# Head sums of a dilated attention as 32-column tiles of TensorE, with heads on partitions in the softmax and the weights turned by DMA

## The chip, the cores and the metric

The kernel runs on one core of one Trainium2 chip. A core has TensorE (PE in the profile: matmuls, with PEld its weight loads), VectorE (DVE), ScalarE (ACT), GpSimd (POOL) and SyncE (SP, which here only issues transfers), and 16 DMA engines that all queues share. The metric is the device time of one execution in microseconds (us), the median of several runs.

## What is computed

One token block of 2048 rows of width 512 goes through a layer norm and then through two branches whose results are added to the input. Branch A is attention with 32 heads of width 16, in which each token looks at 8 earlier tokens, two apart. Branch B is a gated unit with a mix over the sequence.

```python
xn = layernorm(x)                                   # x: 2048 x 512
q, k, v = split(xn @ wqkv)                          # 32 heads of 16
idx = pos[:, None] - 2 * arange(8)[None, :]         # masked where idx < 0
logits = einsum('bhsd,bhswd->bhsw', q, k[idx]) * 16 ** -0.5
a = einsum('bhsw,bhswd->bhsd', softmax(logits), v[idx]) @ wo
z = gelu(xn @ w_in)                                 # 2048 x 1792
z1, z2 = z[..., :896], layernorm(z[..., 896:])
g = einsum('ts,bsf->btf', w_sp, z2) + b_sp[:, None]
out = x + a + (z1 * g) @ w_out
```

## The kernel before

Tokens are cut into 16 blocks of 128 (`b`) and 4 waves of 512 (`j`, and `tc` for the columns of `w_sp`). Every step is a `Task` in a `Plan`: an engine, a function that emits its instructions, the tiles that it reads and writes, an estimated duration `est` and a priority `prio` (lower goes first). `schedule()` runs a list scheduler over the tasks with these estimates and with a simple model of the transfers (an issue time on the queue, a bandwidth, a latency), and the order that comes out for each engine is the order in which that engine's instructions are emitted. `emit()` puts semaphore waits where a task depends on another engine's. So the order on every engine, SP's queue included, is fixed when the kernel is built; on the chip an engine waits at the head of its list. A changed estimate can change the order of everything that follows.

The steps that the change and the prediction touch, with the lines of the kernel before:

- Dummy matmuls (L536 to L541): `NWARM` = 22 matmuls on a tile of zeros, of the lowest priority (`prio` 1000). The first 10 have 512 columns, the other 12 have 128. They read `zeros`, which DVE sets at L492.
- `ln_block` (L550 to L587): statistics and normalization of a block on DVE and POOL. The first 4 blocks are turned by TensorE (L572, evicted by ACT at L578), the other 12 by DMA transposes on SP (L584).
- `v_block` (L589), `qk_pair` (L608), `z2_block` (L689), `z1_group` (L732): the projections. V goes to DRAM (L605). Q and K are laid out with (head, part of the head's width) on partitions: 4 chunks `c` of 4 values of each head, so that partition p belongs to head p // 4.
- `prods` (L627): for each wave, DVE multiplies Q with K shifted by 0, 2, ... 14 tokens (L635, 128 x 4096) for each chunk and adds the 4 products (L640). `pb` then holds, for each of 8 shifts `w`, 512 tokens, and the 4 partitions of a head still have to be summed. TensorE does it with `E32`, a 128 x 32 matrix of zeros and ones (L643 to L652): for each of 4 blocks and 8 shifts the stationary operand is a 128 x 128 piece of `pb`, the moving one is `E32` with 32 columns, so tokens come out on partitions and heads in the columns. That is 32 matmuls in a wave, in two tasks `red`.
- `softmax` (L655 to L687): a mask for the first tokens (first wave only), maximum, subtraction on DVE, exponential on ACT, sum in three steps, reciprocal, and a product (L684) that writes the weights to `attn`, tokens on partitions.
- `pv_block` (L839): for each block the 8 shifted copies of V are loaded from DRAM (L845, 1 MB on SP, 4 slots), multiplied with the weights (L850) and added up (L853, L856) on DVE, and the result is turned by a DMA transpose on SP (L859) into `OT`.
- `g_group` (L811): `w_sp` comes in by 16 DMA transposes on SP (L795), 4 to a wave, in 3 slots of which the third shares its memory with `pb`. 448 matmuls of 512 columns (L822), eviction on ACT (L830), bias and product on DVE (L833, L836).
- `out_block` (L864): 4 matmuls with `wo` (L878) and 7 with `w_out` (L887) for each block, the residual added on DVE (L893), and the store on SP (L898).

The DMA model of the scheduler is this, with `issue` 480 ns for SP and ACT:

```python
xs = max(r + iss + dma_pre, dma_free)
xe = xs + t.dma["nbytes"] / (bw if xs > 7000.0 else min(bw, 265.0))
dma_free = xe
t.end = xe + dma_lat
```

Of the kernel before, what the change touches and what calls it, by code (L numbers as in the profile page):

```python
# [14 lines left out]
NEG_BIG = -1.0e9  # L15
# [21 lines left out]
class Plan:  # L37
# [83 lines left out]
    def schedule(self, dma_bw=300.0, xbar_bw=190.0, dma_lat=1300.0, dma_pre=400.0, issue=None, tol=40.0):  # L121
# [45 lines left out]
        while left:  # L167
# [43 lines left out]
            if t.dma is not None:  # L211
                iss = issue[e]
                t.eng_end = r + iss
                bw = xbar_bw if t.dma.get("xbar") else dma_bw
                xs = max(r + iss + dma_pre, dma_free)
                xe = xs + t.dma["nbytes"] / (bw if xs > 7000.0 else min(bw, 265.0))
                dma_free = xe
                t.end = xe + dma_lat
            else:
                dur = t.est  # L220
                if t.tbl is not None:
                    if tbl is not None and t.tbl != tbl:
                        dur += 1300.0
                    tbl = t.tbl
                t.eng_end = t.end = r + dur
# [103 lines left out]
def build_kernel(nc, A_x, A_wqkv, A_wo, B_x, B_w_in, B_w_sp, B_b_sp, B_w_out, out, report=False, emit=True):  # L329
# [9 lines left out]
    NVS = 4  # L339
    NPB = 3  # L340
    NXT = 4
    NWARM = 22
    x2 = A_x[0]
    o2 = out[0]

# [27 lines left out]

    foff = {}
    fb = 0
    for name, n in (("prime", 4), ("mx", 128), ("Zb", 256), ("Z", 128), ("maskt", 256), ("st6", NB * 6),
                    ("mv", NB * 2), ("vpe", NB), ("rstd", NB), ("s1", NB), ("s2", NB), ("m2", NB), ("msq", NB),
                    ("vpe2", NB), ("rstd2", NB), ("mhalf", 4)):
        foff[name] = fb
        fb += n  # L380
# [5 lines left out]
    with ExitStack() as es:  # L386
# [11 lines left out]
        def Fv(name, n, o2_=0):  # L398
            return fp[:, foff[name] + o2_: foff[name] + o2_ + n]
# [7 lines left out]
        def P(bk, n, o_=0):  # L407
            return ps[:, bk.col(o_): bk.col(o_) + n]
# [71 lines left out]
        ident = A("ident", 128)  # L480
        E32 = A("E32", 32)
        zeros = A("zeros", 512)
        maskt = Fv("maskt", 256)
        mhalf = Fv("mhalf", 4)


# [48 lines left out]

        for wi in range(NWARM):  # L536
            bw = plan.bank("warm%d" % wi)
            n_ = 512 if wi < NWARM - 12 else 128
            T("pe", (lambda bw, n_: lambda t: t.matmul(P(bw, n_), zeros[:, 0:128], zeros[:, 0:n_], start=True,  # L539
                                                       stop=True))(bw, n_),  # L540
              reads=["zeros"], writes=[bw], est=(427.0 if n_ == 512 else 75.0), name="warm%d" % wi, prio=1000)  # L541
# [85 lines left out]
        def prods(j):  # L627
            acc = (0, 2)[j % 2]
            for c in range(4):
                s_ = acc if c == 0 else 1  # L630
                qb = AC(off["QT"] + 2048 * (j % 2) + 512 * c, [[0, 8], [1, 512]])
                kb = AC(off["KT"] + c * (S + KP) + KP + 512 * j, [[-2, 8], [1, 512]])
                pbv = A("pb", 4096, 4096 * s_).rearrange("p (w s) -> p w s", w=8)
                rd = [("QT", c, j % 2), ("KT", c, j), ("KT", c, j - 1) if j > 0 else ("KTpad", c)]
                T("dve", (lambda pbv, qb, kb: lambda v: v.tensor_tensor(pbv, qb, kb, ALU.mult))(pbv, qb, kb),  # L635
                  reads=rd, writes=[("pb", s_)], est=c_tt(4096), name="prod%d_%d" % (j, c), prio=5 + j)
                if c > 0:
                    av = A("pb", 4096, 4096 * acc)
                    bv = A("pb", 4096, 4096 * 1)
                    T("dve", (lambda av, bv: lambda v: v.tensor_tensor(av, av, bv, ALU.add))(av, bv),  # L640
                      reads=[("pb", 1)], writes=[("pb", acc)], est=c_tt(4096), name="padd%d_%d" % (j, c), prio=5 + j)
            bk = plan.bank("lg%d" % j, 2)
            for hf in range(2):  # L643
                def mm(t, hf=hf):
                    last = None
                    for blk in range(2 * hf, 2 * hf + 2):
                        for w in range(8):
                            last = t.matmul(P(bk, 32, blk * 256 + w * 32),  # L648
                                            AC(off["pb"] + 4096 * acc + 512 * w + 128 * blk, [[1, 128]]), E32,
                                            start=True, stop=True)  # L650
                    return last
                T("pe", mm, reads=[("pb", acc), "E32"], writes=[bk], est=16 * 27.0, name="red%d_%d" % (j, hf), prio=1)  # L652
            return bk

        def softmax(j, bk):  # L655
            ds = j % 2
            if j == 0:
                T("dve", lambda v: v.tensor_tensor(P(bk, 256), P(bk, 256), maskt, ALU.add),
                  reads=["maskt"], writes=[bk], est=424, name="smask", prio=4)
            T("dve", lambda v: v.tensor_reduce(Fv("mx", 128).rearrange("p (a h) -> p a h", a=4),  # L660
                                               PC(bk.col(), [[256, 4], [1, 32], [32, 8]]), AX.X, ALU.max),
              reads=[bk], writes=["mx"], est=1218, name="smax%d" % j, prio=4)
            T("dve", lambda v: v.tensor_tensor(A("D", 1024, 1024 * ds).rearrange("p (a w h) -> p a w h", a=4, w=8),
                                               PC(bk.col(), [[256, 4], [32, 8], [1, 32]]),
                                               FCa(foff["mx"], [[32, 4], [0, 8], [1, 32]]), ALU.subtract),
              reads=[bk, "mx"], writes=[("D", ds)], est=1222, name="ssub%d" % j, prio=4)
# [3 lines left out]
            T("dve", lambda v: v.tensor_tensor(A("Za", 512).rearrange("p (a w h) -> p a w h", a=4, w=4),  # L670
                                               AC(do, [[256, 4], [32, 4], [1, 32]]),
                                               AC(do + 128, [[256, 4], [32, 4], [1, 32]]), ALU.add),
              reads=[("D", ds)], writes=["Za"], est=c_tt(512), name="sz1_%d" % j, prio=4)
            T("dve", lambda v: v.tensor_tensor(Fv("Zb", 256).rearrange("p (a w h) -> p a w h", a=4, w=2),
                                               AC(off["Za"], [[128, 4], [32, 2], [1, 32]]),
                                               AC(off["Za"] + 64, [[128, 4], [32, 2], [1, 32]]), ALU.add),
              reads=["Za"], writes=["Zb"], est=423, name="sz2_%d" % j, prio=4)
            T("dve", lambda v: v.tensor_tensor(Fv("Z", 128).rearrange("p (a h) -> p a h", a=4),
                                               FCa(foff["Zb"], [[64, 4], [1, 32]]),
                                               FCa(foff["Zb"] + 32, [[64, 4], [1, 32]]), ALU.add),  # L680
              reads=["Zb"], writes=["Z"], est=292, name="sz3_%d" % j, prio=4)
            T("dve", lambda v: v.reciprocal(A("R", 128), Fv("Z", 128)), reads=["Z"], writes=["R"], est=952,
              name="srec%d" % j, prio=4)
            T("dve", lambda v: v.tensor_tensor(AC(off["attn"] + 1024 * j, [[256, 4], [32, 8], [1, 32]]),  # L684
                                               AC(do, [[256, 4], [32, 8], [1, 32]]),
                                               AC(off["R"], [[32, 4], [0, 8], [1, 32]]), ALU.mult),
              reads=[("D", ds), "R"], writes=[("attn", b) for b in range(4 * j, 4 * j + 4)], est=c_tt(1024), name="sattn%d" % j, prio=4)  # L687

        def z2_block(b):  # L689
            bk = plan.bank("z2_%d" % b, 2)  # L690
# [60 lines left out]
        for b in range(8, NB):  # L751
# [13 lines left out]
        T("pool", lambda g: g.memset(maskt, 0.0), writes=["maskt"], est=310, name="mask0", prio=2, after=lnr[:8])  # L765
        for w in range(1, W):
            T("pool", (lambda w: lambda g: g.memset(fp[0:2 * w, foff["maskt"] + 32 * w: foff["maskt"] + 32 * w + 32],
                                                    NEG_BIG))(w), writes=["maskt"], est=120, name="mask%d" % w, prio=2, after=lnr[:8])
# [70 lines left out]
        def pv_block(b):  # L839
# [126 lines left out]
```

## Time and profile before

| What | Value |
|---|---|
| Median of 3 runs | 239.82 us (239.57, 239.82, 241.82) |
| The profiled execution | 239.45 us, of it 238.0 us from the first to the last instruction |
| TensorE matmuls, busy | 233.0 us, 1211 instructions |
| TensorE weight loads, busy | 112.2 us, beside the matmuls |
| VectorE, busy | 213.3 us, 267 instructions |
| ScalarE, busy | 97.6 us |
| GpSimd, busy | 32.4 us |
| L822, matmuls with the 512 columns of `w_sp` | 98.6 us busy |
| L635, L640, L850, VectorE over 128 x 4096 | 36.6, 27.5 and 36.5 us busy |
| DMA | 42.81 MB, mean 180 GB/s |

The table comes from the profile's page. A busy time of TensorE is the union of its matmuls' durations, and these overlap: a matmul of 512 columns is shown with 379 ns, and in a stream the next one starts well before that. Other engines' times can be added up. In the views of the trace each line gives the start and the duration, the engine, the line of the kernel, the operation and its operands; what stands in square brackets is the idle time of the engine just before it and what ended it.

### The profile page before, as it was taken

The page shows a single profiled execution, that of the slowest core. Times are in us where ns is not written, and L with a number is a line of the kernel's source. Part 1 is how long each engine was busy: PE and PEld are TensorE (multiplying, and loading weights), DVE is VectorE, ACT ScalarE, POOL GpSimd, SP SyncE. Part 2 cuts the span into 40 slices and gives each one's busy share as a digit, 9 for nine tenths or more (in the row PEclk, how much of TensorE's full clock was granted, in tenths as well). Part 3 has the DMA queues.
Part 4 walks back from the last instruction along what each step waited for, and adds up shares of the span by engine and source line. Part 5 has one row for each costly group of instructions (what it writes and reads, how often), then busy time and mean ns, then how long its engine had stood idle before and what let it go on. Part 6 is the DMA issues. An engine that isn't in the chain of part 4 may idle for free.

```text
span 238.0 us, 3156 instructions
## 1 busy us (share of the span) xinstructions
PE 233.0 (98%) x1211; PEld 112.2 (47%) x1233; DVE 213.3 (90%) x267; ACT 97.6 (41%) x144; POOL 32.4 (14%) x56
## 2 busy tenths in 40 slices
PE   7999999999999999999999999999999999999996
PEld 3455555555445444544454444444444444444444
DVE  3889989899989899999999999969999999999962
ACT  2587889899889885631112111101010200101110
POOL 2467250501373500000000000000000000000000
DMA  6999969992437100014079999999999998972112
GB/s 178 365 337 192 190 144 200 215 208 74 110 118 250 56 26 18 0 37 142 0 238 313 190 220 264 194 191 254 283 341 348 272 280 264 245 239 66 22 44 66
DMA packets 77805, 42.81 MB, mean 180 GB/s; under 512 B 50128, under 2 KB 77152, under 8 KB 77792
## 3 DMA queue, kind: packets, MB, share of 16 engines
q1 hardware_dynamic: 76480, 40.13, 69.7%
q0 software_dynamic: 800, 2.11, 2.7%
q10 hardware_dynamic: 512, 0.38, 0.5%
q8 instruction: 9, 0.15, 0.3%
q14 instruction: 4, 0.03, 0.0%
HBM read 26.35 MB, written 4.21 MB: 128 GB/s over the span
## 4 chain that ended last, share of the span: by engine, by line
PE 98%; issue 1%; DVE 0%; ACT 0%
PE ps L822 40%; PE ps L614 12%; PE ps L695 10%; PE ps L887 10%; PE ps L739 10%; PE ps L597 6%; PE ps L878 6%; PE ps L539 2%; PE ps L648 1%; PE ps L572 0%; ACT arena L578 0%; DVE arena L893 0%; DVE arena L492 0%
## 5 line engine op out<-in xcount | busy, mean ns | idle before, releaser
L822 PE MATMUL ps<-arena 128*128 128x512 bf16 x441 | 98.6, 379 | 0.4
L822 PEld LDWEIGHTS ps<-arena 128*128 128x128 bf16 x448 | 43.8, 98 | 52.6
L830 ACT ACTIVATE arena<-ps 128x1024 bf16<-128x1024 f32 (+1 forms) x16 | 14.7, 917 | 106.9 <-PE ps L822 96.3
L635 DVE TENSOR_TENSOR arena<-arena 128x4096 bf16<-128x4096 bf16 x16 | 36.6, 2286 | 0.2
L850 DVE TENSOR_TENSOR arena<-arena 128x4096 bf16<-128x4096 bf16 x16 | 36.5, 2284 | 0.0
L853 DVE TENSOR_TENSOR arena<-arena 128x2048 bf16<-128x2048 bf16 (+1 forms) x32 | 30.6, 955 | 0.6
L614 PE MATMUL ps<-arena 128*128 128x512 bf16 x125 | 28.8, 379 | 0.2
L640 DVE TENSOR_TENSOR arena<-arena 128x4096 bf16<-128x4096 bf16 x12 | 27.5, 2289 | 0.2
L887 PE MATMUL ps<-arena 128*128 128x512 bf16 (+2 forms) x117 | 26.9, 366 | 0.1
L695 PE MATMUL ps<-arena 128*128 128x448 bf16 x128 | 26.0, 352 | 0.0
L739 PE MATMUL ps<-arena 128*128 128x512 bf16 x109 | 24.2, 379 | 0.2
L614 PEld LDWEIGHTS ps<-arena 128*128 128x128 bf16 x128 | 14.5, 113 | 13.0
L893 DVE TENSOR_TENSOR arena<-ps,arena 128x512 bf16<-128x512 f32 (+2 forms) x17 | 11.2, 658 | 8.4 <-PE ps L887 7.3
L623 ACT ACTIVATE arena<-ps 128x1024 bf16<-128x1024 f32 x16 | 16.3, 1020 | 4.5 <-PE ps L614 4.3
L695 PEld LDWEIGHTS ps<-arena 128*128 128x128 bf16 x128 | 12.4, 98 | 11.5
L887 PEld LDWEIGHTS ps<-arena 128*128 128x128 bf16 x119 | 11.6, 98 | 12.7
L739 PEld LDWEIGHTS ps<-arena 128*128 128x128 bf16 x112 | 10.8, 98 | 12.7
L745 ACT ACTIVATE arena<-ps 128x1024 bf16<-128x1024 f32 (+1 forms) x16 | 14.1, 916 | 6.1 <-PE ps L739 6.1
L878 PE MATMUL ps<-arena 128*128 128x512 bf16 (+2 forms) x65 | 16.4, 366 | 0.2
L597 PE MATMUL ps<-arena 128*128 128x512 bf16 x60 | 15.3, 379 | 0.5 <-ACT arena L578 0.3
L701 ACT ACTIVATE arena<-ps 128x896 bf16<-128x896 f32 x16 | 14.6, 913 | 2.6 <-PE ps L695 2.5
L706 ACT ACTIVATE arena<-arena 128x896 bf16<-128x896 bf16 x16 | 15.2, 951 | 0.1
(56 smaller groups left out, 174.5 us busy)
## 6 DMA issues: line engine op xcount, KB each, us to landing
arena<-vscr SPq DMA_DIRECT2D x16, 1024.0 KB, 7.2
arena<-in_A_x_dram SPq DMA_DIRECT2D x29, 128.0 KB, 5.3
vscr<-arena POOLq DMA_DIRECT2D x16, 128.0 KB, 3.2
out_dram<-arena SPq DMA_DIRECT2D x15, 128.0 KB, 3.9
arena<-in_A_wqkv_dram SPq DMA_DIRECT2D x2, 512.0 KB, 6.4
arena<-in_B_w_in_dram SPq DMA_DIRECT2D x2, 448.0 KB, 5.1
arena<-in_B_w_in_dram SPq DMA_DIRECT2D x1, 896.0 KB, 6.0
arena<-in_B_w_out_dram SPq DMA_DIRECT2D x1, 896.0 KB, 5.6
```

Of the source, the lines that this page charges most:

```text
L597: last = t.matmul(P(bk, 512), AC(off["xnT"] + dc * S + 128 * b, [[1, 128]]), AC(off["wv"] + 512 * dc, [[1, 512]]), start=(dc == 0), stop=( ...
L614: last = t.matmul(P(bk, 512, 512 * which), AC(off["wqk"] + 2048 * which + 512 * dc + c, [[4, 128]]), AC(off["xnT"] + dc * S + 512 * j, [[1 ...
L623: T("act", lambda a: a.activation(AC(qo, [[ko - qo, 2], [1, 512]]), P(bk, 1024).rearrange("p (t n) -> p t n", t=2), ACTF.Copy, scale=0.5), ...
L635: T("dve", (lambda pbv, qb, kb: lambda v: v.tensor_tensor(pbv, qb, kb, ALU.mult))(pbv, qb, kb), reads=rd, writes=[("pb", s_)], est=c_tt(40 ...
L640: T("dve", (lambda av, bv: lambda v: v.tensor_tensor(av, av, bv, ALU.add))(av, bv), reads=[("pb", 1)], writes=[("pb", acc)], est=c_tt(4096 ...
L695: last = t.matmul(P(bk, 448, 512 * hf), AC(off["xnT"] + dc * S + 128 * b, [[1, 128]]), AC(off["w_in2"] + 896 * dc + 448 * hf, [[1, 448]]), ...
L739: last = t.matmul(P(bk, 512, 512 * i), AC(off["w_in1"] + 896 * dc + 128 * fc, [[1, 128]]), AC(off["xnT"] + dc * S + 512 * j, [[1, 512]]), ...
L822: last = t.matmul(P(bk, 512, 512 * i), AC(off["z2"] + FH * sh + 128 * fc, [[1, 128]]), AC(off["wT%d" % r_] + sh * 512, [[1, 512]]), start= ...
L850: T("dve", lambda v: v.tensor_tensor(tv, tv, av, ALU.mult), reads=[("attn", b)], writes=[("Vs", sv)], est=c_tt(4096), name="pv%d" % b, pri ...
L853: T("dve", (lambda n: lambda v: v.tensor_tensor(A("Vs", n, 4096 * sv), A("Vs", n, 4096 * sv), A("Vs", n, 4096 * sv + n), ALU.add))(n), wri ...
L878: last = t.matmul(P(bk, cn), AC(off["OT"] + 512 * tb + 128 * cc, [[1, 128]]), AC(off["wo"] + 512 * cc + c0, [[1, cn]]), start=(cc == 0), s ...
L887: last = t.matmul(P(bk, cn), AC(off["z1T"] + fc * S + 128 * tb, [[1, 128]]), AC(off["w_out"] + 512 * fc + c0, [[1, cn]]), start=False, sto ...
```

## The change

- The head sums of a wave become one task of 8 matmuls. `E32` (128 x 32) is now the stationary operand, and 512 columns of `pb` (4 shifts of 128 tokens) are the moving one. Each of the 4 blocks of a wave writes 32 other partitions of PSUM, so the 4 matmuls of one bank stand at 4 column positions of the array. Heads come out on partitions (32 heads of block `a` on partitions 32a to 32a+31), shifts and tokens in the columns.
- The softmax runs in that layout. The mask covers 32 partitions and is written with 128 columns on 32 partitions. The last product works in place in `D`.
- A DMA transpose on SP, 128 x 1024, one in a wave, then turns the weights into `attn`, and `pv_block` reads them with a stride of 128 between shifts.
- There are 23 dummy matmuls (11 with 512 columns and 12 with 128). Their operands are a constant 1.0 of the program in place of `zeros`, so they wait for nothing.
- The scheduler's model of transfers that are issued in the first 5 us is another, and the estimate of the head sums is 600 ns for a wave (before: two tasks of 432 ns).

```diff
-                xs = max(r + iss + dma_pre, dma_free)
-                xe = xs + t.dma["nbytes"] / (bw if xs > 7000.0 else min(bw, 265.0))
+                if r < 5000.0:
+                    xs = max(r + (1300.0 if e == "sp" or r < 1000.0 else 2000.0), dma_free)
+                    fast = max(0.0, t.dma["nbytes"] - max(0.0, 6500.0 - xs) * 275.0)
+                    xe = xs + (t.dma["nbytes"] - fast) / 275.0 + fast / 350.0
+                    t.end = xe + 700.0
+                else:
+                    xs = max(r + iss + dma_pre, dma_free)
+                    xe = xs + t.dma["nbytes"] / bw
+                    t.end = xe + dma_lat
                 dma_free = xe
-                t.end = xe + dma_lat
...
-    NWARM = 22
+    NWARM = 23
...
+        ones = nc.const_aps.tensor(1.0, [128, 512], BF)
...
-            T("pe", (lambda bw, n_: lambda t: t.matmul(P(bw, n_), zeros[:, 0:128], zeros[:, 0:n_], start=True,
+            T("pe", (lambda bw, n_: lambda t: t.matmul(P(bw, n_), ones[:, 0:128], ones[:, 0:n_], start=True,
                                                        stop=True))(bw, n_),
-              reads=["zeros"], writes=[bw], est=(427.0 if n_ == 512 else 75.0), name="warm%d" % wi, prio=1000)
+              writes=[bw], est=(427.0 if n_ == 512 else 75.0), name="warm%d" % wi, prio=1000)
...
-            for hf in range(2):
-                def mm(t, hf=hf):
-                    last = None
-                    for blk in range(2 * hf, 2 * hf + 2):
-                        for w in range(8):
-                            last = t.matmul(P(bk, 32, blk * 256 + w * 32),
-                                            AC(off["pb"] + 4096 * acc + 512 * w + 128 * blk, [[1, 128]]), E32,
-                                            start=True, stop=True)
-                    return last
-                T("pe", mm, reads=[("pb", acc), "E32"], writes=[bk], est=16 * 27.0, name="red%d_%d" % (j, hf), prio=1)
+            def mm(t):
+                last = None
+                for hf in range(2):
+                    for a in range(4):
+                        last = t.matmul(ps[32 * a:32 * a + 32, bk.col(512 * hf):bk.col(512 * hf) + 512], E32,
+                                        AC(off["pb"] + 4096 * acc + 2048 * hf + 128 * a, [[512, 4], [1, 128]]),
+                                        start=True, stop=True)
+                return last
+            T("pe", mm, reads=[("pb", acc), "E32"], writes=[bk], est=600.0, name="red%d" % j, prio=1)
...
-            T("dve", lambda v: v.tensor_reduce(Fv("mx", 128).rearrange("p (a h) -> p a h", a=4),
-                                               PC(bk.col(), [[256, 4], [1, 32], [32, 8]]), AX.X, ALU.max),
+            T("dve", lambda v: v.tensor_reduce(Fv("mx", 128), PC(bk.col(), [[1, 128], [128, 8]]), AX.X, ALU.max),
...
-            T("dve", lambda v: v.tensor_tensor(AC(off["attn"] + 1024 * j, [[256, 4], [32, 8], [1, 32]]),
-                                               AC(do, [[256, 4], [32, 8], [1, 32]]),
-                                               AC(off["R"], [[32, 4], [0, 8], [1, 32]]), ALU.mult),
-              reads=[("D", ds), "R"], writes=[("attn", b) for b in range(4 * j, 4 * j + 4)], est=c_tt(1024), name="sattn%d" % j, prio=4)
+            dv = A("D", 1024, 1024 * ds).rearrange("p (w t) -> p w t", w=8)
+            T("dve", lambda v: v.tensor_tensor(dv, dv, AC(off["R"], [[0, 8], [1, 128]]), ALU.mult),
+              reads=["R"], writes=[("D", ds)], est=c_tt(1024), name="sattn%d" % j, prio=4)
+            dma("sp", lambda e: e.dma_start_transpose(AC(off["attn"] + 1024 * j, [[128, 8], [1, 128]]),
+                                                      A("D", 1024, 1024 * ds)),
+                128 * 1024 * 2, ("attnT", ds), reads=[("D", ds)], writes=[("attn", b) for b in range(4 * j, 4 * j + 4)],
+                name="attnT%d" % j, xbar=True, prio=1)
...
-            av = AC(off["attn"] + 256 * b, [[32, 8], [0, 16], [1, 32]])
+            av = AC(off["attn"] + 1024 * j + 32 * (b % 4), [[128, 8], [0, 16], [1, 32]])
```

Left out of the diff are the mask, the other softmax steps (the same operations on the same number of elements, with plain rows in place of strided ones) and POOL's writing of the mask, where 8 memsets stay 8.

More of the change, by code (lines that the diff above doesn't have):

```diff
@@ L375, in build_kernel @@
     fb = 0
-    for name, n in (("prime", 4), ("mx", 128), ("Zb", 256), ("Z", 128), ("maskt", 256), ("st6", NB * 6),
+    for name, n in (("prime", 4), ("mx", 128), ("Zb", 256), ("Z", 128), ("maskt", 128), ("st6", NB * 6),
                     ("mv", NB * 2), ("vpe", NB), ("rstd", NB), ("s1", NB), ("s2", NB), ("m2", NB), ("msq", NB),
@@ L482, in build_kernel @@
         zeros = A("zeros", 512)
-        maskt = Fv("maskt", 256)
+        ones = nc.const_aps.tensor(1.0, [128, 512], BF)
+        maskt = Fv("maskt", 128)
         mhalf = Fv("mhalf", 4)
@@ L657, in softmax, with msk @@
             if j == 0:
-                T("dve", lambda v: v.tensor_tensor(P(bk, 256), P(bk, 256), maskt, ALU.add),
-                  reads=["maskt"], writes=[bk], est=424, name="smask", prio=4)
-            T("dve", lambda v: v.tensor_reduce(Fv("mx", 128).rearrange("p (a h) -> p a h", a=4),
-                                               PC(bk.col(), [[256, 4], [1, 32], [32, 8]]), AX.X, ALU.max),
+                def msk(v):
+                    lg = bass.AP(tensor=ps, offset=bk.col(), ap=[[PR, 32], [128, 8], [1, 16]])
+                    return v.tensor_tensor(lg, lg, bass.AP(tensor=fp, offset=foff["maskt"],
+                                                           ap=[[FR, 32], [16, 8], [1, 16]]), ALU.add)
+                T("dve", msk, reads=["maskt"], writes=[bk], est=300, name="smask", prio=4)
+            T("dve", lambda v: v.tensor_reduce(Fv("mx", 128), PC(bk.col(), [[1, 128], [128, 8]]), AX.X, ALU.max),
               reads=[bk], writes=["mx"], est=1218, name="smax%d" % j, prio=4)
-            T("dve", lambda v: v.tensor_tensor(A("D", 1024, 1024 * ds).rearrange("p (a w h) -> p a w h", a=4, w=8),
-                                               PC(bk.col(), [[256, 4], [32, 8], [1, 32]]),
-                                               FCa(foff["mx"], [[32, 4], [0, 8], [1, 32]]), ALU.subtract),
+            T("dve", lambda v: v.tensor_tensor(A("D", 1024, 1024 * ds).rearrange("p (w t) -> p w t", w=8),
+                                               PC(bk.col(), [[128, 8], [1, 128]]),
+                                               FCa(foff["mx"], [[0, 8], [1, 128]]), ALU.subtract),
               reads=[bk, "mx"], writes=[("D", ds)], est=1222, name="ssub%d" % j, prio=4)
@@ L669, in softmax @@
             do = off["D"] + 1024 * ds
-            T("dve", lambda v: v.tensor_tensor(A("Za", 512).rearrange("p (a w h) -> p a w h", a=4, w=4),
-                                               AC(do, [[256, 4], [32, 4], [1, 32]]),
-                                               AC(do + 128, [[256, 4], [32, 4], [1, 32]]), ALU.add),
+            T("dve", lambda v: v.tensor_tensor(A("Za", 512), A("D", 512, 1024 * ds), A("D", 512, 1024 * ds + 512),
+                                               ALU.add),
               reads=[("D", ds)], writes=["Za"], est=c_tt(512), name="sz1_%d" % j, prio=4)
-            T("dve", lambda v: v.tensor_tensor(Fv("Zb", 256).rearrange("p (a w h) -> p a w h", a=4, w=2),
-                                               AC(off["Za"], [[128, 4], [32, 2], [1, 32]]),
-                                               AC(off["Za"] + 64, [[128, 4], [32, 2], [1, 32]]), ALU.add),
+            T("dve", lambda v: v.tensor_tensor(Fv("Zb", 256), A("Za", 256), A("Za", 256, 256), ALU.add),
               reads=["Za"], writes=["Zb"], est=423, name="sz2_%d" % j, prio=4)
-            T("dve", lambda v: v.tensor_tensor(Fv("Z", 128).rearrange("p (a h) -> p a h", a=4),
-                                               FCa(foff["Zb"], [[64, 4], [1, 32]]),
-                                               FCa(foff["Zb"] + 32, [[64, 4], [1, 32]]), ALU.add),
+            T("dve", lambda v: v.tensor_tensor(Fv("Z", 128), Fv("Zb", 128), Fv("Zb", 128, 128), ALU.add),
               reads=["Zb"], writes=["Z"], est=292, name="sz3_%d" % j, prio=4)
@@ L764, in build_kernel @@
           prio=2, after=lnr[:8])
-        T("pool", lambda g: g.memset(maskt, 0.0), writes=["maskt"], est=310, name="mask0", prio=2, after=lnr[:8])
+        T("pool", lambda g: g.memset(fp[0:32, foff["maskt"]:foff["maskt"] + 128], 0.0), writes=["maskt"], est=150, name="mask0", prio=2,
+          after=lnr[:8])
         for w in range(1, W):
-            T("pool", (lambda w: lambda g: g.memset(fp[0:2 * w, foff["maskt"] + 32 * w: foff["maskt"] + 32 * w + 32],
-                                                    NEG_BIG))(w), writes=["maskt"], est=120, name="mask%d" % w, prio=2, after=lnr[:8])
+            T("pool", (lambda w: lambda g: g.memset(fp[0:32, foff["maskt"] + 16 * w: foff["maskt"] + 18 * w],
+                                                    NEG_BIG))(w), writes=["maskt"], est=120, name="mask%d" % w, prio=2,
+              after=lnr[:8])
         dma("sp", lambda e: e.dma_start(A("w_in1", 3584).rearrange("p (c n) -> p c n", c=4),
```

## The prediction

> **What bounds the kernel now.** I read the page's busy times and its chain of waits first.
>
> ```profile
> PE 233.0 (98%) x1211; PEld 112.2 (47%) x1233; DVE 213.3 (90%) x267; ACT 97.6 (41%) x144; POOL 32.4 (14%) x56
> ...
> PE 98%; issue 1%; DVE 0%; ACT 0%
> PE ps L822 40%; PE ps L614 12%; PE ps L695 10%; PE ps L887 10%; PE ps L739 10%; PE ps L597 6%; PE ps L878 6%; PE ps L539 2%; PE ps L648 1%; PE ps L572 0%; ACT arena L578 0%; DVE arena L893 0%; DVE arena L492 0%
> ```
>
> TensorE makes up 98% of the chain that ended last, so a microsecond taken from its stream is a microsecond of the kernel, as long as nothing else comes late. DVE is the one that could: 90% busy, with much of the rest at the two ends. The head sums (L648) are 1% of the chain. So the second view is the groups by form, for what a matmul is shown with, and the time-ordered engine view around the last head sums, for what it costs in the stream:
>
> ```profile
> L822 PE MATMUL ps<-arena 128*128 128x512 bf16 x441 | 98.6, 379 | 0.4
> L648 PE MATMUL ps<-arena 128*128 128x32 bf16 x128 | 3.8, 176 | 0.0
> L648 PEld LDWEIGHTS ps<-arena 128*128 128x128 bf16 x128 | 3.7, 96 | 1.1 <-DVE arena L640 0.7
> ```
> ```profile
> 122.49 0.95 PE L648 MATMUL ps<-arena 128*128 128x32 bf16 x32
> 123.29 3.40 PE L822 MATMUL ps<-arena 128*128 128x512 bf16 x14
> ```
>
> A wave's 32 small matmuls occupy the stream from 122.49 to 123.29, 0.80 us or 25 ns each; the 0.95 shown holds the tail of the last, which overlaps its successor. Likewise a 512-column matmul is shown with 379 ns, but the chain in order of time has pieces such as 12 of them in 2.59 us: 216 ns each, so 163 ns of each lie beside the next. Third, the chain at the start, where the dummies are:
>
> ```profile
> 0.92 0.28 DVE arena L492
> ...
> 1.25 4.55 PE ps L539 x16
> 5.80 0.24 PE ps L572 x4
> 6.04 0.02 issue
> 6.07 0.39 ACT arena L578
> ```
> ```profile
> 5.62:12.00 6.38, 6.01 (x46) 3.25 (x45) 5.25 (x16) 3.30 (x7) 2.85 (x5) 1.00 1.10 366
> 126.00:160.00 34.00, 33.84 (x157) 15.37 (x158) 30.59 (x35) 4.72 (x5) 0.00 (x0) 1.00 1.12 224
> ```
>
> The columns of the second fence are the stretch, its length, busy PE, PEld, DVE, ACT and POOL, clock, DMA share, GB/s. Fourth, the SP queue and what waits for its transfers:
>
> ```profile
> 159.91 1.27 SPq L859 DMA_TRANSPOSE arena<-arena  x1
> ...
> 162.94 1.27 SPq L859 DMA_TRANSPOSE arena<-arena  x1
> ```
> ```profile
> arena<-arena SPq DMA_TRANSPOSE x1, 5.6
> ```
> ```profile
> 169.26 1.03 PE L878 MATMUL ps<-arena 128*128 128x512 bf16 x4
> ```
>
> The transpose issued at 162.94 took 5.6 us to land, at 168.5, and the output matmuls that read it start at 169.26: 0.75 us of slack, the least of the 16 blocks (others: 1.0 to 3.7).
>
> **The change, part by part.** *Head sums.* Taken away: 4 waves x 0.80 = 3.2 us of the stream. Added: 8 matmuls of 512 columns in a wave. No row shows a 32-column tile, so the bounds are: at best the four positions of a PSUM bank run at once, two rounds of 216 ns, 0.43 us; at worst nothing runs at once and the pipeline empties at both ends, 8 x 216 + 2 x 163 = 2.05 us. So a wave lies between 0.37 us less and 1.25 us more than now, the kernel between -1.5 and +5.0 us. I take 0.60 us: two rounds and one emptying of the pipeline (0.43 + 0.163), near the low end, because the four matmuls write disjoint partitions and their shares of the array are disjoint. That is 4 x (0.60 - 0.80) = -0.8 us. Break-even is at 0.80/0.216 = 3.7 matmul times for the eight.
>
> The row behind the 163 ns is the 379 ns shown against the 216 ns of the stream. On this the Trainium skill (TensorEngine Tiling (Array Packing), Key Properties) says that tiles at different positions work in parallel, but that a change of the tiling mode drains the engine; every wave enters and leaves the mode, so the rule speaks against part of the gain. For the size of the gain the skill (TensorE: Matmul & The Clock Gate, Measured speedup vs the span model) gives 2.38 times for 3 column tiles and 3.07 times for 4 row tiles; by the latter a wave would be an estimated 8 x 216/3.07 = 563 ns, and the sum -1.0 us. No trace here shows either.
>
> *Softmax on DVE.* The same 1024 elements per partition in the same operations: 1.22 us (L660 and L663), 0.42, 0.42, 0.29, 0.95 and 0.69 each wave. The mask falls from 128 to 32 partitions and from 256 to 128 columns, at 0.43 us now, once. The maximum reads PSUM with a stride of 128 values where it was 32; between no change and one more pass of 1.22 us a wave I take no change. The cover: DVE sits idle for PE in front of the residuals (L893) 7.3 us in all. Cost without cover: 4.9 us of DVE.
>
> *Transposes of the weights.* Four more transfers on SP, 256 KB each. Nearest rows: 128x512 takes 1.2 us to issue and at least 2.4 to land (L859), 128x2048 from DRAM 1.9 to 2.3 us and at least 4.3 (L795, uncrowded). So 1.2 to 2.3 us of SP each, some 1.5. Who waits for the data is far off: the weights of waves 0 to 3 are done at 59.7, 86.8, 111.6 and 131.8, and the first products that read them (L850) start at 126.7, 153.4, 179.8 and 204.2, 67 us later at the least. The reuse of `D` two waves on has 38 us (86.8 to 124.7). What is queued behind: the first three fall where SP issues nothing urgent (the next issues are at 62.6, 105.1 and 119.7, and DMA is nearly idle before the last two). The fourth falls between the transposes of `w_sp` for the third and fourth column wave, where the DMA share is 1.12 and single issues on SP last up to 8.3 us. There it pushes back what follows by 1.2 to 2.3 us, less what the new order, made with this transfer in it, puts in between. I take zero and keep 1.55 us (2.3 less the 0.75 of slack) for the range.
>
> *Dummies.* They can start at 0.92, when DVE starts today, in place of 1.25. But the first transposes (L572) need block 0 normalized, which DVE ends at 5.56 (5.15 and 0.41 long), and they start at 5.64: the dummies end just then. They are spaced 0.43 us, the last ones 55 ns. With an earlier start and one more of the long ones, 11 x 0.43 end at 5.65 even if all stay slow, so 0 to 0.1 us, and nothing if the fast spacing comes as early as now. I take 0. An order with other places for the short dummies can win at most what PE wastes between 5.62 and 12.00: 6.38 - 6.01 = 0.37 us idle and six dummies, 0.34 us, together 0.7. POOL's 8 memsets are off the path.
>
> *Sum.* -0.8 + 0 + 0 + 0: the profiled execution would go from 239.45 to 238.65. It stands 0.37 under the median of 239.82, so I forecast 239.0.
>
> **Rivals.** (a) *The change of mode eats the gain.* Emptying at both ends, 2 x 163 ns, and the first weights on either side not loaded beside other matmuls, 2 x 96 ns: 0.43 + 0.33 + 0.19 = 0.95 us a wave, +0.15. Four waves: 239.8 + 0.6 = 240.4; with only the emptying (0.76) 239.7. For it: today the row of weight loads shows them beside matmuls throughout. Against: the pipeline's tail may fill while the next weights go in. The drain cited above is this rival.
>
> (b) *The tiles do not run at once*, which is also the way in which the change does not do what it says. 8 x 216 = 1.73 us a wave, +0.93, or +1.25 with the emptying: 243.5 to 244.8. It decides from 3.7 matmul times on. For it: no matmul of this trace overlaps another one's streaming, and all have one common spacing. Against: all of them use the whole array, so the trace cannot show it.
>
> (c) *The fourth transpose makes the loads late.* In place: SP after 131.9. V for block 5 (issued 151.44, 8.7 us, landed 160.1) is read at 160.79, 0.65 us later; the turned block 3 has 0.75. Pushed by 1.2 to 2.3 us, PE stalls for 0.45 to 1.55: 239.4 to 240.6 with the gain of the head sums. If SP then sits behind a full queue once more, as in its issues of 4.5 and 7.8 us at 143.49 and 152.06, it is up to 4 us: 243. Against: PE's order there can hold other matmuls (L822) that are ready, and after 160 DVE idles for PE by 0.3 to 0.4 us six times, which takes up 2.1 us.
>
> (d) *The start gains too:* up to 0.7 us beside a gain of 0.8 to 1.5: 237.6 to 238.3.
>
> **Chances.** Forecast (0.43 to 0.60 a wave, 238.3 to 239.0, up to 239.3 with small losses) 38%; (a) 20%; (b) 15%; (c) 17%, a third of it above 242.2; (d) 8%; anything else 2%. A change of 1% (2.4 us) is about what a measurement tells from none. Faster by over 1% is under 237.4, which no case reaches unless the start wins more than it wastes now: 5%. Slower by over 1% is (b), a third of (c) and a little more: 22%. Within 1%: 73%. The range 237.5 to 242.6 takes in everything but (b), the top of (c) and the rest, 19 to 20%. The likeliest case's own range is 238.3 to 239.3.
>
> **What would show it.** In the order view, from the start of a wave's head sums to the next group: under 0.65 us my step, 0.75 to 1.0 (a), over 1.7 (b). Four transposes of `arena` on SP of about 1.5 us; a wait of L878 for DMA, or of L850 for the V loads, after 155 is (c). L572 starting at 5.6 as now, and less idle time up to 12.0 than 0.37 us, is (d). DVE rows L660 and L663 staying at 1.22 us hold the softmax step. I am wrong if PE falls clearly under 98% of the chain, or if a wave of head sums costs more than 1 us.

## The result, and the profile after

| | before | after |
|---|---|---|
| Median of the runs made side by side (22 each) | 240.28 us | 241.08 us |
| Lowest and highest run | 239.50, 241.82 | 240.67, 241.55 |
| The profiled execution (its span) | 239.45 us (238.0) | 241.03 us (239.5) |

After takes 1.0031 times as long as before, with an interval of 1.0017 to 1.0045: 0.8 us slower by the medians, where 0.8 us faster was forecast. The time is inside the range and the change within 1%, but it goes the other way than forecast, and the interval doesn't contain 1. (In all ratios here the runs of before are those of the same rounds, so a ratio need not be exactly the quotient of two medians.) The two profiled executions differ by more than the medians, by 1.58 us: the one of before is near the low end of its spread, the one of after is at its median. The account below is between these two profiles, so some 0.8 us of it is the low draw of before.

The busy times and the chain of waits on the page after:

```profile
span 239.5 us, 2970 instructions
...
PE 233.2 (97%) x1116; PEld 109.3 (46%) x1138; DVE 212.9 (89%) x267; ACT 97.5 (41%) x144; POOL 32.7 (14%) x56
...
PE 58%; DVE 27%; POOL 9%; issue 3%; DMA 2%; ACT 0%; DVEq 0%; POOLq 0%
```

The busy times have hardly moved; the chain has. TensorE fell from 98% of it to 58%, and 27% is DVE, 9% POOL: the chain now runs through the layer norms and products on DVE up to the third head sums and only then on TensorE. That is the sign that the prediction named for being wrong. Where it changes over is seen around the third head sums, in the chain after in order of time (start, duration, what):

```profile
94.24 2.30 DVE arena L642
96.55 0.02 issue
96.57 2.30 DVE arena L647
98.87 0.14 issue
99.01 0.61 PE ps L655 x8
99.62 1.83 PE ps L746 x8
```

TensorE's own list at that place, after and then before (start, duration, group, idle time before it):

```profile
91.78 5.99 PE L746 MATMUL ps<-arena 128*128 128x512 bf16 x26
99.01 0.61 PE L655 MATMUL ps<-arena 128*32 128x512 bf16 x8 [1.24 <-DVE arena L647]
99.56 1.90 PE L746 MATMUL ps<-arena 128*128 128x512 bf16 x8
```
```profile
91.73 6.64 PE L739 MATMUL ps<-arena 128*128 128x512 bf16 x30
98.37 0.97 PE L648 MATMUL ps<-arena 128*128 128x32 bf16 x32
99.40 0.81 PE L739 MATMUL ps<-arena 128*128 128x512 bf16 x3
```

Before, 30 matmuls of the gate projection stand ahead of the third sums and 3 behind (one record is missing); after, 26 and 8: the sums stand one task of 4 matmuls further ahead. The last one ahead starts at 97.39 after (91.78 + 5.99 - 0.38, the duration of one), and the sums at 99.01, 1.62 us later; where nothing waits the two starts are 0.31 us apart. So 1.31 us are lost. Before, the two starts are 0.38 us apart (97.99 and 98.37), where the old form has 0.22 when nothing waits (122.27 and 122.49 at the fourth sums): there TensorE already waited 0.16 us. The products that the sums need end at 98.87 after; before, DVE starts its next step at 98.23, after at 98.78, so it is 0.55 us later too. Some 0.1 us of this is chance: in the profiles taken below, DVE is there at 98.01 to 98.53 in the order of before and at 98.64 to 98.78 in that of after. TensorE arrives earlier at a step for which DVE is later.

The second place is the end, here the chain's last stretch after:

```profile
230.53 1.21 PE ps L896 x6
231.74 2.90 DMA arena<-arena
234.64 0.05 issue
234.69 0.72 PE ps L887 x4
```

The last block's attention output is finished by DVE at 231.71 (before: at 228.92) and has to be turned by a transfer. TensorE runs out of other matmuls and stands 0.65 us from its last start to 234.69, where 0.22 is normal: 0.43 us lost. Before, the chain goes through this place without a wait:

```profile
230.94 0.86 PE ps L878 x4
231.80 1.51 PE ps L887 x7
233.31 0.54 PE ps L878 x4
```

That DVE is 2.8 us later there began far earlier. DVE's rows for two residuals, after and before:

```profile
159.56 0.69 DVE L902 TENSOR_TENSOR arena<-ps,arena 128x512 bf16<-128x512 f32 x1 [0.78 <-PE ps L896]
...
168.84 0.69 DVE L902 TENSOR_TENSOR arena<-ps,arena 128x512 bf16<-128x512 f32 x1 [2.87 <-PE ps L896]
```
```profile
160.18 0.69 DVE L893 TENSOR_TENSOR arena<-ps,arena 128x512 bf16<-128x512 f32 x1 [2.33 <-PE ps L887]
...
166.87 0.69 DVE L893 TENSOR_TENSOR arena<-ps,arena 128x512 bf16<-128x512 f32 x1 [0.28 <-PE ps L887]
```

In TensorE's list of after 32 matmuls of `w_sp` stand ahead of the second of these output blocks (159.36 to 166.26), in that of before 20 (159.98 to 164.30). DVE reaches the residual, has nothing else that its list allows, and idles 2.87 us. At the first of the two it idles less than before, so together it loses 1.0 us more (3.65 against 2.61). The product (L859, before L850) behind the second residual starts at 169.44, before at 167.48, and from there on DVE stays behind by 0.8 to 3.7 us: its last product starts at 224.34, before at 222.25.

The head sums themselves did what was forecast, and so did the rest: the softmax rows L670 and L672 on DVE are 1.22 and 1.23 us as before, the first transposes start at 5.61 (before 5.64), and two of the weights' transposes occupy SP so:

```profile
112.06 1.24 SPq L691 DMA_TRANSPOSE arena<-arena  x1
...
140.70 1.35 SPq L691 DMA_TRANSPOSE arena<-arena  x1
```

The account between the two profiles: head sums 4 x -0.16 = -0.64 (worked out below); third sums +1.15 (1.31 lost in place of 0.16); second sums +0.18 (starts 0.49 apart, 0.31 when nothing waits); the end +0.43. The first 48 us, up to the first sums, are 0.4 us longer (the matmul ahead of them starts at 47.90, before at 47.52). Together +1.5, and the spans differ by 239.5 - 238.0 = 1.5. The 0.4 us are chance in the main: in the profiles below that keep the order of before, this matmul starts at 47.49 to 47.88. So the sums and the waits make up 1.1 of the 1.5 us.

### The profile page after: what moved, and what is told of

The parts are those of the page before. It is cut to its first block, busy times and chain, and to the rows that moved or that the text cites. A ratio compares the mean times of both kernels' runs of the same rounds, so it can differ in the third digit from the quotient of the medians.

```text
span 239.5 us, 2970 instructions
## 1 busy us (share of the span) xinstructions
PE 233.2 (97%) x1116; PEld 109.3 (46%) x1138; DVE 212.9 (89%) x267; ACT 97.5 (41%) x144; POOL 32.7 (14%) x56
## 4 chain that ended last, share of the span: by engine, by line
PE 58%; DVE 27%; POOL 9%; issue 3%; DMA 2%; ACT 0%; DVEq 0%; POOLq 0%
PE ps L831 40%; PE ps L896 9%; DVE arena L642 9%; DVE arena L647 7%; PE ps L887 5%; POOL fpool L729 5%; DVE arena L732 3%; POOL fpool L567 2%; DVE arena L569 2%; DMA arena<-arena 1%; DMA arena<-in_A_x_dram 1%; DVE arena L672 1%; DVE fpool L670 1%; DVE arena L686 1%; PE ps L604 1%
## 5 line engine op out<-in xcount | busy, mean ns | idle before, releaser
L859 DVE TENSOR_TENSOR arena<-arena 128x4096 bf16<-128x4096 bf16 x16 | 36.5, 2283 | 0.0
```

## The experiments

Theory one, from these views: the steps are right and the *order* costs. The list scheduler planned anew, with one task of sums in place of two, a price for each transpose in its single model of the DMA, and the new model of the first transfers; its order sends TensorE early to places where DVE is late. Its rivals: the sums in their new form cost more elsewhere (weight loads that nothing hides, the change of mode), the transposes hold up other transfers (theory 2 in the expectations), or the dummies and the start are worse. Where an order had to be held, the list scheduler's choice was replaced by a fixed list:

```diff
-            pick = None
-            for e in ENGS:
...
+            t = byname[ORDER[len(self.tasks) - left]]
```

with `ORDER` the list of tasks in the order of the kernel before or after, and the PSUM banks from a table of that kernel.

**New sums in the old order.** The kernel after, with order, banks and dummies of before; the two tasks of sums are merged at the place of the first, each weights' transpose stands right behind its last softmax step.

> The new head sums, softmax and the four transposes of the weights, with every other instruction in the order (and PSUM banks) of the kernel before, its dummies and its scheduler's model; only the transposes are added to SP's list, each right behind the product that it waits for. Theory 1 (the order is what costs): four head sums save 4 x 0.25 us on PE and the order of before keeps DVE as early as before, so 0.3 to 1.0 us under the kernel before. Theory 2 (the transposes delay the loads of V and with them DVE, whatever the order): at or above the changed kernel, 0.5 to 1.5 us over the kernel before.

Measured: 239.26 us (238.95 to 239.66), 0.9959 of before, 0.9941 to 0.9977. The new sums alone win 0.4%. (By the lowest runs it is 0.40 us, 238.95 against 239.35; by the medians it is more because the runs of before spread further up.) At the third sums TensorE waits 0.25 us here (98.05 to 98.61, where 0.31 is the least). Nothing waits at the fourth sums, and the group's cost can be read from TensorE's list:

```profile
120.75 1.89 PE L856 MATMUL ps<-arena 128*128 128x512 bf16 x8
122.57 0.62 PE L680 MATMUL ps<-arena 128*32 128x512 bf16 x8
123.12 2.12 PE L856 MATMUL ps<-arena 128*128 128x512 bf16 x9
```

The last matmul ahead starts at 122.26 (120.75 + 1.89 - 0.38), the first behind at 123.12. Without a group these would be 0.216 us apart, so the group costs 0.86 - 0.216 = 0.64 us. The same reckoning for before gives 0.80. Four waves: -0.64 us.

**Old sums in the new order.** The kernel before, with the order, banks and dummies of after, without transposes.

> The reverse: head sums, softmax and layout of the kernel before, no transposes of the weights, with the order, PSUM banks, dummies and scheduler's model of the changed kernel. Theory 1: slower than the changed kernel by what the sums save, that is 1.0 to 2.0 us over the kernel before. Theory 2: as the kernel before, within 0.4 us.

Measured: 240.99 us (240.82 to 241.38), 1.0038, 1.0022 to 1.0053, with not one of the new sums or transposes in it. The third sums again start late, 1.45 us behind the last start before them:

```profile
98.89 0.95 PE L686 MATMUL ps<-arena 128*128 128x32 bf16 x32 [1.07 <-DVE arena L678]
```

So the loss is the order's: the first two runs and the two kernels make a square of sums and order, in which the new order costs 0.4% with the old sums and 0.7% with the new ones (1.0031 against 0.9959, the dummies too being others), and the new sums win 0.4% in the old order and 0.1% in the new one (1.0031 against 1.0038), which the runs don't tell from nothing: there DVE sets the pace.

**Dummies alone.** Before, with 23 dummies on the constant.

```diff
-    NWARM = 22
+    NWARM = 23
...
+        ones = nc.const_aps.tensor(1.0, [128, 512], BF)
```

> The kernel before with the 23 dummies on the constant alone; the order of all else is unchanged. If the dummies matter: a median 0.2 to 0.7 us under the kernel before and a narrower spread of its runs, because an earlier busy TensorE is at full speed in all runs when the first transposes come. If they do not: within 0.2 us, with the same spread of about 2 us.

Measured: 239.76 us (239.41 to 241.47), 0.9988, 0.9967 to 1.0009. No effect that can be told. Together with the new sums in the old order, the constant (with 22 dummies) gives 239.11 us:

> As e1 (new sums in the order of before), with the 22 dummies on the constant, so that they start 0.3 us earlier. The best of the parts together: at e1 or up to 0.3 us under it, 0.6 to 1.2 us under the kernel before. The dummies do nothing if it is e1 within 0.2 us.

Measured: 238.98 to 239.22 over 5 runs, 0.9939, 0.9917 to 0.9960. This is faster than both kernels. Against the first experiment the difference, 0.15 us by the medians, is within what the intervals leave open.

**What made the order another?** First the scheduler's inputs one by one. The model of the first transfers and the dummies set back in the kernel after:

> The new sums, softmax and transposes in an order that the scheduler makes itself, with the old model of the transfers and the old dummies. Theory 1, if the new model of the first transfers is what spoils the order: at or under the kernel before (0 to 1.0 us less). Theory 1, if already the new tasks spoil it: 0.5 to 2 us over the kernel before, with TensorE waiting for DVE before the third head sums or at the last output. Theory 2: 0.5 to 1.5 us over it, with waits for loads of V between 150 and 175.

Measured: 241.28 us, 1.0044, 1.0026 to 1.0061. As slow, but elsewhere: at the third sums TensorE loses 0.44 us (starts 0.75 apart), with 4 matmuls behind them as before, and at the end 1.5 (starts 1.72 apart, 0.22 being normal). Next, a price of zero for the transposes in the scheduler, from there:

```diff
-                128 * 1024 * 2, ("attnT", ds), reads=[("D", ds)], ...
+                0, ("attnT", ds), reads=[("D", ds)], ...
```

> As e4 (new sums, old model of the transfers, old dummies, the scheduler's own order), but the scheduler is told that the four transposes of the weights move 0 bytes; what runs on the chip is the same instructions in another order, with SP's order as in the kernel before. If it is the price of the transposes in the scheduler that spoils the order: 1.0 to 2.0 us under e4, that is 0.3 to 0.8 us under the kernel before. If the new sums alone (another length, one task for two) spoil it: at e4, about 1.2 us over the kernel before.

Measured: 239.70 us, 0.9980, 0.9962 to 0.9998. The wait at the end is gone, the starts at the third sums are 0.75 apart as they were. The transposes are on the chip as before; only their price in the plan is zero. The model alone, in the kernel before:

> The kernel before with the new model of the first transfers alone, no other instruction changed. It puts the statistics of block 3 behind the normalization of block 2. If that order costs DVE 0.7 us that come back at the end: 0.4 to 1.0 us over the kernel before. If PE has slack for it: within 0.3 us.

Measured: 239.95 us, 1.0001, 0.9977 to 1.0025: no change. The price alone, in the kernel after:

> The changed kernel whole, with 0 bytes for the four transposes in the scheduler. If their price is the larger of the two causes: 0.6 to 1.5 us under the changed kernel, and over e5 by what the new model of the first transfers costs (0 to 0.7 us). If the model is the larger: within 0.4 us of the changed kernel, about 0.8 us over the kernel before.

Measured: 240.52 us, 1.0005, 0.9984 to 1.0026. The wait at the end goes, the one at the third sums stays (starts 1.61 apart). The two losses have separate sources. The one at the end comes with the price of the transposes. The larger part of the one at the third sums comes with the new model of the transfers and the dummies (0.44 us with the old ones, 1.3 with the new), but not with the model alone, which costs the kernel before nothing. Whether the dummies or the new sums have to come with it was not tried.

**Which place in the list costs?** DVE's lateness was first sought in the layer norms, where after takes `norm2` ahead of the statistics of block 3. In the order of after with these two exchanged:

```diff
-warm15 V0_1 ldx9 norm1 warm16 ldx10 Ve0 warm17 warm18 warm19 bnag2 xTr1 vpe2 warm20 ldx11 rstd2 xTe1_0 warm21 warm22 z2_0_0 ldx12 norm2 ldx13 bnst3
+warm15 V0_1 ldx9 norm1 warm16 ldx10 Ve0 warm17 warm18 warm19 bnag2 xTr1 vpe2 warm20 ldx11 rstd2 xTe1_0 warm21 warm22 z2_0_0 ldx12 bnst3 norm2 ldx13
```

> The changed kernel in its own order, but for one swap on DVE: the statistics of block 3 before the normalization of block 2, as in the kernel before. If the late layer norm is what puts DVE behind: DVE's first head-sum maximum 0.5 to 0.8 us earlier, TensorE's wait before the third head sums shorter by the same, and the time 0.3 to 0.8 us under the changed kernel. If DVE's later order decides alone: within 0.2 us of the changed kernel.

Measured: 240.97 us, 1.0028, 1.0005 to 1.0051: a miss. DVE's last norm starts at 29.79, after at 29.92, before at 29.22. The 0.13 us are no effect that can be told, for the other profiles in the order of after have 29.66 to 29.91; the gap at the third sums stays 1.62. What makes DVE late in the norms was not isolated. By itself it needn't cost: in the kernel with the model alone the last norm starts at 29.70, and the third sums wait for nothing, because its order brings DVE to the next step at 97.69.

Next the other side, TensorE's place for the third sums. The order of after with `red2` two tasks (8 matmuls) later, behind `z1_5_3` and `z1_6_3`; that is one task later than in the kernel before:

```diff
-z1_4_3 z1g2_3 prod3_0 red2 z1_5_3 z1_6_3 z1g4_3 smax2 g0_0_0 z1g6_3 g0_0_1 ssub2 g0_0_2 prod3_1 sexp2 g0_0_3 g1_0_0 g1_0_1 padd3_1 ldVs1 g1_0_2 g1_0_3
+z1_4_3 z1g2_3 prod3_0 z1_5_3 z1_6_3 red2 z1g4_3 smax2 g0_0_0 z1g6_3 g0_0_1 ssub2 g0_0_2 prod3_1 sexp2 g0_0_3 g1_0_0 g1_0_1 padd3_1 ldVs1 g1_0_2 g1_0_3
```

> The changed kernel in its own order, but for one task on TensorE: the third wave's head sums stand behind the 8 matmuls of L746 that followed them. If TensorE's wait of 1.3 us there is a loss of its own: the gap before the sums shrinks to 0.3, and the time is 0.8 to 1.3 us under the changed kernel (about 240.0). If DVE, at the end, sets the time whatever TensorE does in the middle: within 0.3 us of the changed kernel, and the wait comes back before the last output.

Measured: 239.85 us, 0.9976, 0.9952 to 1.0001. That wins 1.2 us by the medians, about the 1.3 that were lost there. The chain around the third sums has no DVE in it any more:

```profile
94.96 4.53 PE ps L777 x21
99.49 0.55 PE ps L686 x8
100.03 3.13 PE ps L862 x14
```

The wait for the turned block at the end is still there. Both edits together, the price of zero and the sums later:

> As e13, with the order that the scheduler makes when the four transposes cost it nothing (as in e7, where the wait at the end was gone and the one before the third sums stayed). If the two waits are the whole loss: as e8, 0.6 to 1.0 us under the kernel before. If something else in the changed kernel's order costs: 0.3 to 0.6 us over e8.

Measured: 239.29 us, 0.9964, 0.9941 to 0.9986. The last stretch of its chain, where after had the transfer:

```profile
231.49 0.86 PE ps L927 x4
232.35 0.05 issue
232.41 0.59 PE ps L927 x2
233.00 0.54 PE ps L918 x4
```

| medians, us | sums early | sums later |
|---|---|---|
| transposes priced in the plan | 241.08 | 239.85 |
| transposes at zero in the plan | 240.52 | 239.29 |

The two add up: -1.23 and -0.56, together -1.79. Both are edits of the order alone. But for the place of the sums, the list with the price of zero is that of after up to the products of block 3 (at 146.71 after) and differs only from there, so the two edits act at different places. The last kernel with the old order and the sums one task later:

> As e8 (new sums in the order of before, constant dummies), with the third wave's head sums one task later on TensorE, where it waits 0.25 us. If TensorE bounds there: up to 0.25 us under e8. If DVE is now the bound: e8 within 0.15 us.

Measured: 238.99 us (238.50 to 239.24), 0.9953, 0.9930 to 0.9976, 0.12 us under the 239.11 of the old order. TensorE waited 0.25 us for these sums there (starts 0.56 apart), and here it waits for nothing (0.31 apart); the runs don't tell a gain of this size from none.

**Is DVE really a second bound?** The kernel before with two more operations on DVE behind the last norm (an addition of 1024 elements whose result nobody reads; one of the two is shown):

```diff
+            T("dve", lambda v: v.tensor_tensor(A("D", 1024), A("w_in1", 1024), A("w_in1", 1024), ALU.add),
+              reads=["w_in1"], writes=[("D", 0)], est=685, name="extra0")
```

> The kernel before in its own order, with two more DVE instructions of 0.69 us each behind the last normalization (at 29 us); their result is not used. If DVE is as much a bound as TensorE: 0.7 to 1.4 us over the kernel before, with TensorE waiting for DVE before the second and third head sums. If TensorE alone bounds, as the prediction took it: within 0.3 us.

Measured: 242.15 us (241.30 to 243.41), 1.0072, 1.0042 to 1.0102. Two operations of 0.69 us cost 1.7 us (by the ratio) to 1.9 us (by the medians). That is no less than the 1.4 us that they last, which lies inside the interval (1.0 to 2.45 us), and more than the 0.7 to 1.4 expected. The chain of this kernel is like after's:

```profile
PE 61%; DVE 27%; POOL 9%; issue 1%; ACT 1%; DVEq 0%
```
```profile
PE ps L679 <- DVE arena L671: 1.3, 3, 0.8
```

The second fence is the view of waits (us in total, times, longest): the head sums wait for DVE. So in the kernel before DVE stood right behind TensorE, with 7.3 us of idle time elsewhere that was no help.

**The rival of the transposes.** The old order with every transpose of the weights issued twice:

```diff
+            dma("sp", lambda e: e.dma_start_transpose(AC(off["attn"] + 1024 * j, [[128, 8], [1, 128]]),
+                                                      A("D", 1024, 1024 * ds)), ..., name="attnU%d" % j)
```

> As e8, with each of the four transposes of the weights done twice, one behind the other. If the transposes themselves cost nothing on the chip (the prediction's zero): within 0.2 us of e8. If the fourth makes the loads of V late (theory 2): 0.4 to 1.5 us over e8.

Measured: 240.51 us, 1.0014, 0.9990 to 1.0039, 1.4 us over the 239.11 of the same kernel with one set. TensorE waits for a turned block:

```profile
148.04 1.02 PE L916 MATMUL ps<-arena 128*128 128x512 bf16 x4 [1.03 <-DMA arena<-arena]
```

The mechanism of that rival exists, and the first set stays within the slack. It isn't what made after slower: in after no output block waits for a transfer until the last, and there because DVE was late with the block itself.

**Do neighbours in the list have to stand at different positions?** The two loops of a group exchanged, so that two matmuls of the same 32 columns follow each other:

```diff
-                for hf in range(2):
-                    for a in range(4):
+                for a in range(4):
+                    for hf in range(2):
```

> As e8, with the two loops over the 8 matmuls of a wave exchanged, so that each two neighbours stand at the same column position and the next two at another. If four positions at once make the short group: the group goes from 0.55 us (first to next stream matmul) to 1.0 to 1.2 (five rounds of 0.22), and the kernel gains nothing over the kernel before or loses 0.5. If a group is short for another reason: it stays at 0.55.

Measured: 238.97 us (238.87 to 240.18), 0.9960, 0.9932 to 0.9988, unchanged: a miss. The group's list:

```profile
122.21 0.63 PE L680 MATMUL ps<-arena 128*32 128x512 bf16 x8
122.77 2.55 PE L856 MATMUL ps<-arena 128*128 128x512 bf16 x11
```

Again 0.56 us from its start to the next. In the trace four of the eight start within 0.02 us at 122.21 and four at 122.44, as in the other order. The trace doesn't name the position of a matmul, and all eight at one position weren't tried. So the runs show what the group costs, and not that the four positions are the reason.

## Why the prediction failed

**Head sums: right, and sized right.** Taken: 0.60 us a wave, -0.8 in all. Measured: 0.64 us, -0.64. From a group's start to the next matmul it is 0.55 us, under the 0.65 named for the step. Rivals (a) at 0.75 to 1.0 and (b) above 1.7 fall. The parts are others than those of the sum, though: the starts on either side of a group stand 0.31 us apart against 0.216, so entering and leaving cost 0.1 us each, where the sum had one emptying of 0.163. That the totals lie so close is partly luck. The Trainium skill (TensorEngine Tiling (Array Packing), Key Properties) says that a change of the tiling mode drains the engine; this agrees with the 0.1 us at either end, though no run separates the drain from other causes. The 563 ns of the prediction's estimate are 0.08 us under the 0.64 measured.

**Softmax on DVE: right.** Taken: no change, on rows of 1.22 us; they are 1.22 and 1.23.

**Dummies: right.** Taken: 0. They start at 0.84 in place of 1.25, and the first transposes still wait for DVE's first norm (5.14 + 0.42): 5.61. Rival (d) did not happen.

**Transposes on the chip: right.** Taken: 1.5 us of SP each and no delay. They take 1.23 to 1.35 us in after, and rival (c) isn't the loss, though four more of them cost 1.4 us.

**The order: the step that failed.** That a changed estimate can change the order of everything that follows stood in the description of the kernel, and the prediction spoke of the new order only as something that helps: as put "in between" to soften the fourth transpose, as holding other matmuls against rival (c), and as "an order with other places for the short dummies". It started from "a microsecond taken from its stream is a microsecond of the kernel, as long as nothing else comes late", named DVE as the one that could, and gave neither the order nor a late DVE a term in the sum. The runs price the order at 0.4% to 0.7%, against 0.4% won by the sums where the order is kept. No reason for the zero is given; the nearest to one is the sentence on cover, that DVE idles 7.3 us in front of the residuals. That idle time lies behind TensorE in a fixed list, after 150 us, and the head sums that wait for DVE lie before 125 us. On the way to those, DVE had next to no room: 1.4 us more of work there cost 1.7 to 1.9 us. What should have been read is the distance between TensorE and DVE at each of the four sums: at the third the starts stood 0.38 us apart, 0.22 being the least of that form. TensorE already waited there, so whatever brought it earlier or DVE later was lost.

**The sign.** The rival on the other side that came true was not among those listed. It would have been: the new plan lets TensorE reach one head sum a task of 4 matmuls (4 x 0.216 = 0.86 us) earlier while DVE stays; then all of it is waited for, and the kernel is 0.86 - 0.64 = 0.2 us slower, or some 0.8 with the 0.55 us by which DVE is later in the profile after.

**What stays open.** The runs of before spread over 2.3 us (239.50 to 241.82), those of after over 0.9 us, and the 10 of the old order with the sums later over 0.7 us (the 5 with the sums in their old place over 0.2). The constant alone didn't narrow it (239.41 to 241.47). Part of it goes with the granted clock: of the 113 runs of before made beside the experiments 12 took more than 241.3 us, and 10 of these show a clock of 0.996 to 0.998, where all 22 runs of after show 1.0. Why it differs wasn't found. Nor was it settled which part of the new order makes the norms on DVE late (the last one starts at 29.66 to 29.92 in it, at 28.99 to 29.51 in the old order).

## What to carry to other kernels

Where a program plans the order of all engines from estimates, a change of an estimate is a change of the whole kernel: hold the order fixed to measure an edit, then let the plan move and measure that by itself. Before calling a second engine's idle time cover, look where it lies: between two engines of about 90% and 98% busy, each handover has its own slack, and in this kernel the smallest one decided. A kernel with the new sums, the old order and the dummies on the constant is 0.4% to 0.8% faster than before; the edit was good and its plan was not.

## What the hardware showed

- Eight matmuls with 32 stationary columns, two at each of four positions, start in two fours in the trace, the second four 0.21 to 0.23 us behind the first, and it is the same when the program lists the two of one position next to each other. The eight of 512 columns then cost 0.64 us of the stream, where eight of the usual form take 1.73 (8 x 0.216).
- At each change into or out of that form the distance between starts is 0.1 us longer (0.31 against 0.216).
- Transposing 128 x 1024 from the core's memory into itself keeps SP for 1.23 to 1.35 us in after. With one set of four no output block but the last waits for a transfer; a second set costs 1.4 us.
